# Linear attention and a balanced expert layer: the attention's TensorE work put in the order in which its loads arrive

## The chip, the cores and the metric

The kernel runs on one NeuronCore of a Trainium2 chip. The metric is the device time in microseconds (us) of one execution. The engines of the core work side by side: TensorE (PE, matrix products; its weight loads are shown as PEld), VectorE (DVE), ScalarE (ACT), GpSimd (POOL) and SyncE (SP), whose queue issues the large transfers. TensorE writes to PSUM, and VectorE and ScalarE take results from there to SBUF.

## The reference

Two blocks follow one another. Batch 8, 8 heads, 576 positions, head size 64; all inputs are float32.

```python
kv = np.einsum('bhsd,bhse->bhde', k, v)
out = np.einsum('bhsd,bhde->bhse', q, kv)
rms = np.sqrt(np.mean(out * out, axis=-1, keepdims=True) + 1e-06)
x = (out / rms * g_norm)            # then (batch, head, position, d) -> (batch*position, head*d): 4608 x 512

logits = x @ w_gate                 # 4608 tokens, 8 experts
# tokens are given to experts in the order of all logits, largest first,
# with room for 4608 / 8 = 576 tokens at each expert
for e in range(E):
    h = np.maximum(x[mask_e] @ w1[e], 0.0)     # w1: 512 x 1024
    out[mask_e] = h @ w2[e]                    # w2: 1024 x 512
```

## The kernel before, in words

**Stages.** First the attention for all eight batches, which leaves the normalised rows in a DRAM buffer `x_dram` and the logits in SBUF (`lg`). Then a search for the first expert's threshold, then eight experts one after the other. The change concerns the attention alone.

**Loads.** q, k and v of a batch come in two halves each (`load`, L83): half h has the heads of pairs 2h and 2h+1, 576 KB. All are issued on SP's queue. `paced` (L75) makes each transfer of that queue wait for the one issued three before it, so three are under way at a time. Each half has two buffers, so a batch's buffers serve the batch two later: `again` (L381) issues the load of batch b+2 where the last reader of batch b is issued. The first two batches are loaded at the kernel's start in the order of L92.

**Preparing a batch** (`Prepare`, L373). A pair of heads is one "r" of four.
- `sum_kv` (L406): for each pair 18 matmuls in four 64x64 quadrants (36 records, since each float32 product is two passes) into `kv_ps`; even blocks of positions are summed on one half of the partitions, odd ones on the other.
- `add_halves` (L416): ScalarE copies the odd half (`odd`), VectorE adds it to the even half (`kv`), and GpSimd copies `kv` to both halves of the partitions of `kvx`.
- `turn` (L386): 18 transposes of q, in groups of four (the last, group 4, of two), into a PSUM tile with tag "tr" (two buffers), then a copy to `qt`: groups 1 and 2 by VectorE, 0, 3 and 4 by ScalarE.
- `turn_kv` (L426) transposes kv, in the free half of group 4's PSUM tile, and ScalarE copies that to `kvt`.
- `gate` (L434) multiplies `kvt` with the gate's weights `gw` (already scaled by `g_norm`); eight matmuls, since the result is needed on both halves of the partitions. It lies in free columns of the tile's own PSUM buffer. `keep_gate` (L440) copies it into the last 8 columns of each head in `kvx`: one product with q then gives a head's output and its share of the logits together.

**A group of tiles.** A batch has four tiles of 128 positions, and every second batch a fifth, whose two halves of rows belong to two batches (the "split row": its matmuls are 64x64). `product` (L505) makes one tile, 8 matmuls (16 records) into `o_ps` (two buffers); `square` (L526) squares on ScalarE and sums on VectorE; `keep` (L533) copies the tile to `o_sb`. At the end of the group `scale` and `logits` take the root and the reciprocal, sum the logits, and let GpSimd scale the rows (`xo`) for the write to `x_dram`.

**Order.** The queues of TensorE, VectorE, ScalarE and SP are in the order in which the code issues (`manual_schedule`, L582). `prepare_first` (L445) prepares batch 0. In the loop over the batches, `between` (L462) puts steps of the next batch, and the sums of the one after that, behind each tile: behind the first tile pair 2 and transposes 0, behind the second pair 3, the addition and transposes 1, behind the third transposes 2 and 4 with kv's, and pair 0 of the batch after; the gate comes with the fourth tile (n == 3), transposes 3 and pair 1 behind the last. `ones(n)` (L358) issues n matmuls of 128x128 on 512 columns of ones, whose result nobody reads. `chore` (L352) issues the next piece of small VectorE work for the later search. `writes` holds the transfers to `x_dram`.

Of the kernel before, what the change touches and what calls it, by code (L numbers as in the profile page):

```python
# [7 lines left out]
FT = mybir.dt.float32  # L8
# [7 lines left out]
P = 128  # L16
# [10 lines left out]
def kernel(  # L27
# [24 lines left out]
    W = D + E  # L52
# [12 lines left out]
    att = att_cm.__enter__()  # L65
# [17 lines left out]
    def load(name, b, h):  # L83

        loaded[name, b, h] = att.tile([P, NP // 2, R, D], FT, name=f"{name}_sb", tag=name + str(h), bufs=2)
        rs = slice(h * NP // 2, (h + 1) * NP // 2)
        src = {"k": k, "v": v, "q": q}[name]
        paced(nc.sync.dma_start(
            loaded[name, b, h].rearrange("p r j d -> p r (j d)"),
            src[b].rearrange("h s d -> (h s) d").rearrange("(r p j) d -> p r (j d)", r=NP, j=R)[:, rs]))  # L90

    for b, order in enumerate(("kvqkvq", "kvkvqq")):  # L92
        for n, name in enumerate(order):
            load(name, b, int(name in order[:n]))

# [7 lines left out]
    gw = const.tile([P, NP, 2, E], FT, name="gw")  # L103
# [125 lines left out]
    for st in range(1, NSTEP):  # L229
        n = (1.0 + 2 * FUZZ) / (NCAND + 1) if 1 < st <= DIGITS else 1.0 / (NCAND + 1)  # L230
# [4 lines left out]
    for st in range(1, NSTEP):  # L235
        n = (1.0 + 2 * FUZZ) / (NCAND + 1) if st <= DIGITS else 1.0 / (NCAND + 1)
# [131 lines left out]
    kv_ps = psa.tile([P, 2, 512], FT, name="kv_ps", tag="kv")  # L368
    odds = kv_ps[D:P, :, 0:NP * D]
    evens = kv_ps[0:D, :, 0:NP * D].rearrange("p l (r d) -> p l r d", d=D)  # L370
    OW = NP * W

    class Prepare:  # L373

# [11 lines left out]
        def turn(self, *which):  # L386
            NT = NP * R // 2
            if self.qt is None:
                self.qt = turned_q[self.b] = att.tile([P, 2, NT, HP], FT, name="qt", tag="qt", bufs=2)
            for n in which:  # L390
                m = min(4, NT - 4 * n)
                q_ps = pst.tile([P, 4, P], FT, name="qt_ps", tag="tr")
                for x in range(m):
                    h, at = divmod(4 * n + x, NT // 2)
                    nc.tensor.transpose(q_ps[:, x, :], self.q_sb[h][:, at * P:(at + 1) * P], ident)  # L395
                if n == 4:
                    self.turn_kv(q_ps[:, m:4])
                to, got = self.qt[:, :, 4 * n:4 * n + m], q_ps[:, 0:m].rearrange("p x (l c) -> p l x c", l=2)
                if n in (1, 2):
                    nc.vector.tensor_copy(to, got)  # L400
                else:
                    nc.scalar.copy(to, got)
                if n in (2, 3):
                    self.again("q", n - 2)

        def sum_kv(self, *which):  # L406
            for r in which:
# [18 lines left out]
        def turn_kv(self, beside):  # L426

            t_ps = beside.rearrange("p x c -> p (x c)").rearrange("p (r d) -> p r d", d=D)
            for r in range(NP):
                nc.tensor.transpose(t_ps[:, r, :], self.kv[:, r].rearrange("p l d -> p (l d)"), ident[0:D, 0:D])  # L430
            self.kvt = att.tile([P, NP, D], FT, name="kvt", tag="kvt")
            nc.scalar.copy(self.kvt, t_ps)

        def gate(self, beside):  # L434
            for r in range(NP):
                for n in range(2):
                    nc.tensor.matmul(beside[n * D:(n + 1) * D, r // 2, OW + r % 2 * 2 * E:OW + (r % 2 + 1) * 2 * E],
                                     lhsT=self.kvt[:, r, :], rhs=gw[:, r].rearrange("p l e -> p (l e)"), start=True, stop=True)

        def keep_gate(self, beside):  # L440
            nc.scalar.copy(self.kvx[:, :, D:W].rearrange("p (b h) e -> p b h e", b=2),
                           beside[:, :, OW:OW + NP * E].rearrange("p b (h e) -> p b h e", e=E))
            kv_of[self.b] = self.kvx

    def prepare_first():  # L445

        one = Prepare(0)
        one.sum_kv(0, 1)
        ones(2)
        one.turn(0)  # L450
        ones(6)
        one.sum_kv(2, 3)
        one.add_halves()
        one.turn(1)
        ones(5)
        one.turn(4, 2, 3)
        nc.vector.tensor_scalar(gw.rearrange("p r l e -> p (r l e)"), in0=gw.rearrange("p r l e -> p (r l e)"),
                                scalar1=g_col, scalar2=None, op0=AL.mult)
        one.gate(kv_ps)
        one.keep_gate(kv_ps)  # L460

    def between(n, one, two, count):  # L462

        first = one.b == 1
        if n == 0:
            if first:
                ones(2)
                one.sum_kv(0, 1)
            else:
                one.sum_kv(2)  # L470
                one.turn(0)
        elif n == 1:
            if first:
                one.sum_kv(2)
            one.sum_kv(3)
            one.add_halves()
            one.turn(0 if first else 1)
        elif n == 2:
            if first:
                one.turn(1)  # L480
            one.turn(2, 4)
            if two:
                two.sum_kv(0)
        if n == count - 1:
            one.turn(3)
            if two:
                two.sum_kv(1)

    HELD = 6
    writes, late = [], []  # L490
# [90 lines left out]
    PE, DVE, ACTE, SPE = (mybir.EngineType.PE, mybir.EngineType.DVE, mybir.EngineType.Activation, mybir.EngineType.SP)  # L581
    with tc.manual_schedule(engines={PE, DVE, ACTE, SPE}):  # L582
        ones(18)
        prepare_first()
        preparing = {1: Prepare(1)}
        for b in range(B):
            following = preparing.pop(b + 1, None)
            if b + 2 < B:
                preparing[b + 2] = Prepare(b + 2)
            rows = [((b, j), (b, j + 2)) for j in (0, 1, 4, 5)]  # L590
            if b % 2:
                rows.append(((b - 1, R - 1), (b, R - 1)))
            product, square, keep, scale, logits = tiles(b // 2 * R + b % 2 * (R // 2), rows)
            if b in choose_at:
                early(*choose_at[b])
            order = range(len(rows)) if b % 2 == 0 else [len(rows) - 1] + list(range(len(rows) - 1))
            for n, t in enumerate(order):
                at_end = n if b + 1 == B else 0
                o_ps = product(t, 1 if b == 0 and n in (0, 3) else 0, at_end)
                if following and n == 3:  # L600
                    following.gate(o_ps)
# [12 lines left out]
            logits()  # L614
            if b < 4:
                chore()

            while b in (B - 4, B - 3) and writes:
                writes.pop(0)()
        early(27, GC)  # L620
        while chores:
            chore()
        for do in late:
            do()
        while writes:
            writes.pop(0)()
# [21 lines left out]
    for nm, shape in (("n", (E, G)), ("all", (3, E)), ("a", (GC + 2,)), ("s", (NB, GC + 3))):  # L648
        n = shape[0] * (shape[1] if len(shape) > 1 else 1)
# [737 lines left out]
```

## Time and profile before

| | |
|---|---|
| median of 3 runs | 645.37 us (643.71 to 659.32) |
| the profiled execution's own time | 648.04 us |
| its span, first to last instruction | 646.3 us |
| mean granted TensorE clock | 0.956 |
| attention: first tile, start of the last group, last tile's end | 19.3, 108.2, 113.3 us |
| start of the experts' dense stage | about 150 us |
| TensorE busy, 41 to 63.9 us | 22.9 of 22.9 us |
| HBM read, written | 71.3 MB, 18.9 MB |

The profile's page is of one execution. A "slice" is a fortieth of the span, 16.2 us. "PEclk" is the clock that TensorE was granted, in tenths of full speed. In a timeline each row is a run of like instructions, with its start, its length, the engine, the line, output and inputs, the number, and in brackets the engine's idle time before it with what ended that. "issue" there is idle time that no semaphore explains. Rows of neighbouring groups overlap by about 0.07 us, as the ends of matmuls are modelled; the distance from start to start is the cost of a group.

### The profile page before, as it was taken

To read this page: it belongs to the slowest core of one execution; us is meant where nothing else is said; L and a number is where in the kernel's file an instruction comes from. 1 tells how busy PE (TensorE), PEld (TensorE's weight loads), DVE (VectorE), ACT (ScalarE), POOL (GpSimd) and SP (SyncE) were. 2 spreads that over 40 slices of the span, in tenths; PEclk is the share of its full clock that TensorE was granted. 3 is DMA by queue.
4 is the path that set the end of the run, shared out by engine and by line. 5 is a ranking of instruction groups with operands and counts; after the bars stand their busy time and mean duration, and the time that the engine had idled before them with its cause. 6 is when DMAs were issued, how large, how long until landed. Compare 5 with 4: busy or idle time off the path is not lost.

```text
span 646.3 us, 12765 instructions
## 1 busy us (share of the span) xinstructions
PE 606.6 (94%) x4909; PEld 470.3 (73%) x4913; DVE 378.9 (59%) x1234; ACT 203.9 (32%) x440; POOL 385.8 (60%) x402
## 2 busy tenths in 40 slices
PE   8899999339999999999999999999999999999994
PEld 4688888225787678777867786778678777867873
DVE  4356769777887778579658857966662062132101
ACT  1447667932221232213122312231232123122310
POOL 1133553006775598479739873887498579849822
PEclk9869999558999999999999999999999999999998
DMA  8999998338108206310911091017104420910001
GB/s 277 298 318 307 296 319 327 136 112 250 55 19 316 73 2 235 115 59 1 310 57 42 18 316 42 34 61 273 42 32 161 173 73 1 320 54 33 2 9 65
DMA packets 49852, 91.02 MB, mean 141 GB/s; under 512 B 3712, under 2 KB 20096, under 8 KB 49792
## 3 DMA queue, kind: packets, MB, share of 16 engines
q1 hardware_dynamic: 43200, 71.31, 32.3%
q0 software_dynamic: 5888, 18.88, 8.5%
q8 instruction: 39, 0.64, 0.4%
q14 instruction: 21, 0.17, 0.1%
q10 hardware_dynamic: 704, 0.02, 0.1%
HBM read 71.32 MB, written 18.87 MB: 140 GB/s over the span
## 4 chain that ended last, share of the span: by engine, by line
PE 81%; DVE 9%; issue 5%; DMA 2%; ACT 1%; POOL 1%; POOLq 0%; SPq 0%; DVEq 0%; ACTq 0%
PE x_ps L1203 13%; PE x_ps L1163 12%; PE z_ps L1203 9%; PE y_ps L1203 9%; PE y_ps L1163 8%; PE z_ps L1163 7%; PE o_ps L520 4%; PE y_ps L1265 4%; PE kv_ps L411 3%; PE t_ps L1105 3%; PE qt_ps L395 3%; DMA v_sb<-in_v_dram 2%; PE given_ps L717 1%; PE warm_ps L947 1%; PE given_ps L712 1%
## 5 line engine op out<-in xcount | busy, mean ns | idle before, releaser
L1208 ACT COPY h<-x_ps 128x288 f32<-128x288 f32 x93 | 37.2, 400 | 165.9 <-PE x_ps L1203 159.5
L1203 PE MATMUL x_ps<-xs,sw 128*128 128x288 f32 x248 | 71.4, 409 | 0.4 <-DVE xs L1118 0.4
L1130 POOL DMA_INDIRECT out_dram<-y_sb,outs x32 | 31.5, 985 | 56.5 <-DVE y_sb L1301 41.0
L1163 PE MATMUL x_ps<-tw,sh 128*128 128x256 f32 x256 | 61.5, 384 | 0.0
L1203 PEld LDWEIGHTS x_ps<-xs,sw 128*128 128x128 f32 x248 | 46.1, 190 | 13.5 <-issue 1.1
L1110 ACT ACTIVATE xt<-t_ps,g_col 128x512 f32<-128x512 f32 (+3 forms) x41 | 25.8, 635 | 91.4 <-PE t_ps L1105 91.2
L564 POOL TENSOR_TENSOR xo<-o_sb,inv 128x512 f32<-128x512 f32 x27 | 28.4, 1082 | 40.5 <-DVE inv L551 36.3
L1155 POOL TENSOR_TENSOR sh<-hid 128x512 f32<-128x512 f32 x32 | 40.7, 1271 | 19.8 <-ACT hid L1178 19.8
L1163 PEld LDWEIGHTS x_ps<-tw,sh 128*128 128x128 f32 x256 | 47.0, 190 | 7.0 <-issue 0.8
L1091 POOL TENSOR_TENSOR sw<-w_sb 128x256 f32<-128x256 f32 x64 | 46.8, 731 | 7.7 <-PE z_ps L1203 7.3
L1178 ACT ACTIVATE hid<-hid 128x576 f32<-128x576 f32 x64 | 43.8, 686 | 22.7 <-DVE hid L1217 12.6
L1013 POOL DMA_INDIRECT xg<-x_dram,ids x40 | 38.2, 954 | 15.6 <-issue 9.9
L1241 POOL TENSOR_TENSOR tw<-w_sb 128x512 f32<-128x512 f32 x32 | 40.0, 1273 | 6.6 <-DMA w_sb<-in_moe_w_dram 6.6
L520 PE MATMUL o_ps<-kvx,qt 64*128 64x72 f32 (+1 forms) x624 | 40.7, 281 | 0.6 <-issue 0.4
L531 DVE TENSOR_REDUCE ms<-sq 128x8 f32<-128x512 f32 x36 | 24.4, 682 | 26.8 <-ACT sq L530 26.2
L520 PEld LDWEIGHTS o_ps<-kvx,qt 64*128 64x128 f32 (+1 forms) x624 | 35.5, 187 | 4.9 <-issue 3.7
L1203 PE MATMUL z_ps<-xt,sw 128*128 128x288 f32 x128 | 38.0, 414 | 0.0
L1203 PE MATMUL x_ps<-xt,w_sb 128*128 128x288 f32 x124 | 37.3, 415 | 0.5 <-ACT xt L1110 0.5
L1203 PE MATMUL y_ps<-xt,w_sb 128*128 128x288 f32 x128 | 36.8, 408 | 0.0
L1203 PE MATMUL z_ps<-xs,sw 128*128 128x288 f32 x128 | 36.8, 409 | 0.0
L1203 PE MATMUL y_ps<-xs,w_sb 128*128 128x288 f32 x128 | 36.5, 407 | 0.0
L1295 ACT COPY u<-x_ps 128x512 f32<-128x512 f32 x24 | 14.0, 584 | 66.3 <-PE x_ps L1163 52.6
(315 smaller groups left out, 1337.4 us busy)
## 6 DMA issues: line engine op xcount, KB each, us to landing
w_sb<-in_moe_w_dram SPq DMA_DIRECT2D x32, 512.0 KB, 5.6
w_sb<-in_moe_w_dram SPq DMA_DIRECT2D x8, 2048.0 KB, 12.5
k_sb<-in_k_dram SPq DMA_DIRECT2D x16, 576.0 KB, 5.6
v_sb<-in_v_dram SPq DMA_DIRECT2D x16, 576.0 KB, 5.6
q_sb<-in_q_dram SPq DMA_DIRECT2D x16, 576.0 KB, 6.2
x_dram<-xo SPq DMA_DIRECT2D x16, 512.0 KB, 4.1
x_dram<-xo SPq DMA_DIRECT2D x4, 256.0 KB, 3.5
xg<-x_dram,ids POOLq DMA_INDIRECT x40, 5.1
```

The source lines that it names most:

```text
L520: nc.tensor.matmul(o_ps[rows_at, rp, (2 * r2 + l) * W:(2 * r2 + l + 1) * W], lhsT=turned_q[bn][ks, l, block // 2:block // 2 + m].rearrange ...
L564: nc.gpsimd.tensor_tensor(xo[:, t], o_sb[:, t, :, 0:D], inv[:, t * H:(t + 1) * H].rearrange("p (h o) -> p h o", o=1).to_broadcast([P, H, D ...
L1013: tokens = nc.gpsimd.indirect_dma_start(out=xg[0:nr], out_offset=None, in_=x_dram, in_offset=bass.IndirectOffsetOnAxis(ap=ids[0:nr, n:n + ...
L1091: in_order(nc.gpsimd.tensor_tensor(o, x, y, op=op))
L1130: put = nc.gpsimd.indirect_dma_start(out=out, out_offset=bass.IndirectOffsetOnAxis(ap=ids_of[t][0:nr, n:n + 1], axis=0), in_=y_sb[0:nr, :] ...
L1155: in_order(nc.gpsimd.tensor_tensor(o[:, ms], x[:, ms], y[:, ms], op=op))
L1163: nc.tensor.matmul(p_ps[:, n], lhsT=left[:, f, n * P:(n + 1) * P], rhs=right[:, f], start=first, stop=(f == FH - 1), skip_group_check=True)
L1178: nc.scalar.activation(both, both, ACT.Relu)
L1203: nc.tensor.matmul(p_ps, lhsT=lhs[:, r], rhs=rhs[:, r], start=(m in (1, 2, 4, 5) and r == 0), stop=(r == 1), skip_group_check=(m in (6, 7, ...
L1208: nc.scalar.copy(u, p_ps)
L1241: in_order(nc.gpsimd.tensor_tensor(o, x, y, op=AL.subtract))
L1265: nc.tensor.matmul(y_ps[l * nr:(l + 1) * nr], lhsT=hid[:, l * FH + f, a:a + nr], rhs=w2[:, l * FH + f, :], start=(f == 0), stop=(f == FH - 1))
```

## The change

Four things are changed.

1. **Order of batch 0's loads**: k, v, k, v, q, q instead of k, v, q, k, v, q.
2. **Order of the steps**: `between` and the second batch of look-ahead are gone. Behind tile n of a group comes pair n of the next batch (and behind the first tile the present batch's transposes 4); behind the fourth pair the addition. After the last tile's `keep` come transposes 0 and 1, kv's transposes, a wide matmul of ones after even batches, the gate, and transposes 2 and 3, and only then `scale` and `logits`. In odd batches the split row is second instead of first. Batch 0 is prepared in the same order. The second half of q is loaded again behind transposes 4 instead of 3.
3. **The gate**: kv's transposes and the gate have places of their own in the banks of `kv_ps`. `kvt` holds its columns twice, so that one matmul of 128 weight columns gives both halves of the partitions: four matmuls instead of eight.
4. **Chores and writes**: the chores are issued at other tiles, and the first writes to `x_dram` are issued behind the first tile of batch 5 instead of the end of batch 4.

```diff
-    for b, order in enumerate(("kvqkvq", "kvkvqq")):
+    for b, order in enumerate(("kvkvqq", "kvkvqq")):
...
-    OW = NP * W
+    t_ps = kv_ps[:, 0, NP * D:2 * NP * D].rearrange("p (r d) -> p r d", d=D)
+    w_ps = kv_ps[:, 1, NP * D:NP * (D + 2 * E)].rearrange("p (r e) -> p r e", r=NP)
...
-                if n == 4:
-                    self.turn_kv(q_ps[:, m:4])
...
-                if n in (2, 3):
-                    self.again("q", n - 2)
+                if n in (2, 4):
+                    self.again("q", n // 2 - 1)
...
-            self.kvt = att.tile([P, NP, D], FT, name="kvt", tag="kvt")
-            nc.scalar.copy(self.kvt, t_ps)
+            self.kvt = att.tile([P, NP, 2, D], FT, name="kvt", tag="kvt")
+            nc.scalar.copy(self.kvt, t_ps.rearrange("p r (o d) -> p r o d", o=1).to_broadcast([P, NP, 2, D]))
...
+        def gate(self):
+
             for r in range(NP):
-                for n in range(2):
-                    nc.tensor.matmul(beside[n * D:(n + 1) * D, r // 2, OW + r % 2 * 2 * E:OW + (r % 2 + 1) * 2 * E],
-                                     lhsT=self.kvt[:, r, :], rhs=gw[:, r].rearrange("p l e -> p (l e)"), start=True, stop=True)
...
+                nc.tensor.matmul(w_ps[:, r], lhsT=self.kvt[:, r].rearrange("p n d -> p (n d)"),
+                                 rhs=gw[:, r].rearrange("p l e -> p (l e)"), start=True, stop=True)
+            nc.scalar.copy(self.kvx[:, :, D:W], w_ps.rearrange("p r (l e) -> p (r l) e", l=2))
...
         one.sum_kv(0, 1)
         ones(2)
-        one.turn(0)
-        ones(6)
         one.sum_kv(2, 3)
         one.add_halves()
-        one.turn(1)
         ones(5)
-        one.turn(4, 2, 3)
+        one.turn_kv()
+        one.turn(0, 1)
         nc.vector.tensor_scalar(gw.rearrange("p r l e -> p (r l e)"), in0=gw.rearrange("p r l e -> p (r l e)"),
                                 scalar1=g_col, scalar2=None, op0=AL.mult)
-        one.gate(kv_ps)
-        one.keep_gate(kv_ps)
+        one.gate()
+        ones(2)
+        one.turn(2, 3)
+        return one
...
-            order = range(len(rows)) if b % 2 == 0 else [len(rows) - 1] + list(range(len(rows) - 1))
+            order = (0, 1, 2, 3) if b % 2 == 0 else (0, 4, 1, 2, 3)
             for n, t in enumerate(order):
                 at_end = n if b + 1 == B else 0
-                o_ps = product(t, 1 if b == 0 and n in (0, 3) else 0, at_end)
-                if following and n == 3:
-                    following.gate(o_ps)
+                o_ps = product(t, 1 if b < 2 and n in (0, 3) else 0, at_end)
                 square(t, o_ps)
-                if following and n == 3:
-                    following.keep_gate(o_ps)
-                if following:
-                    between(n, following, preparing.get(b + 2), len(rows))
+                if n == 0:
+                    here.turn(4)
+                if following and n < NP:
+                    following.sum_kv(n)
+                    if n + 1 == NP:
+                        following.add_halves()
                 keep(t, o_ps, at_end)
-                if b < 2 or b == 6 or n in (1, 3):
+                if n + 1 < len(order) and (b < 2 or b == 6 or n in (1, 3)):
                     chore()
-            if b + 1 == B:
+                while (b, n) == (B - 3, 0) and writes:
+                    writes.pop(0)()
+            if following:
+                following.turn(0, 1)
+                following.turn_kv()
+                if b % 2 == 0:
+                    ones(1)
+                following.gate()
+                following.turn(2, 3)
+            else:
                 while chores:
                     chore()
             scale()
             logits()
+            if b % 2 == 0 or b < 2:
+                chore()
             if b < 4:
                 chore()
-            while b in (B - 4, B - 3) and writes:
+            while b == B - 3 and writes:
                 writes.pop(0)()
+            here = following
```

More of the change, by code (lines that the diff above doesn't have):

```diff
@@ L424, in add_halves, with turn_kv @@
                 nc.gpsimd.tensor_copy(self.kvx[n * D:(n + 1) * D, :, 0:D], self.kv.rearrange("p r l d -> p (r l) d"))
-        def turn_kv(self, beside):
-            t_ps = beside.rearrange("p x c -> p (x c)").rearrange("p (r d) -> p r d", d=D)
+        def turn_kv(self):
             for r in range(NP):
                 nc.tensor.transpose(t_ps[:, r, :], self.kv[:, r].rearrange("p l d -> p (l d)"), ident[0:D, 0:D])
-            self.kvt = att.tile([P, NP, D], FT, name="kvt", tag="kvt")
-            nc.scalar.copy(self.kvt, t_ps)
-        def gate(self, beside):
+            self.kvt = att.tile([P, NP, 2, D], FT, name="kvt", tag="kvt")
+            nc.scalar.copy(self.kvt, t_ps.rearrange("p r (o d) -> p r o d", o=1).to_broadcast([P, NP, 2, D]))
+        def gate(self):
             for r in range(NP):
-                for n in range(2):
-                    nc.tensor.matmul(beside[n * D:(n + 1) * D, r // 2, OW + r % 2 * 2 * E:OW + (r % 2 + 1) * 2 * E],
-                                     lhsT=self.kvt[:, r, :], rhs=gw[:, r].rearrange("p l e -> p (l e)"), start=True, stop=True)
-        def keep_gate(self, beside):
-            nc.scalar.copy(self.kvx[:, :, D:W].rearrange("p (b h) e -> p b h e", b=2),
-                           beside[:, :, OW:OW + NP * E].rearrange("p b (h e) -> p b h e", e=E))
+                nc.tensor.matmul(w_ps[:, r], lhsT=self.kvt[:, r].rearrange("p n d -> p (n d)"),
+                                 rhs=gw[:, r].rearrange("p l e -> p (l e)"), start=True, stop=True)
+            nc.scalar.copy(self.kvx[:, :, D:W], w_ps.rearrange("p r (l e) -> p (r l) e", l=2))
             kv_of[self.b] = self.kvx
@@ L449, in prepare_first @@
         ones(2)
-        one.turn(0)
-        ones(6)
         one.sum_kv(2, 3)
         one.add_halves()
-        one.turn(1)
         ones(5)
-        one.turn(4, 2, 3)
+        one.turn_kv()
+        one.turn(0, 1)
         nc.vector.tensor_scalar(gw.rearrange("p r l e -> p (r l e)"), in0=gw.rearrange("p r l e -> p (r l e)"),
                                 scalar1=g_col, scalar2=None, op0=AL.mult)
-        one.gate(kv_ps)
-        one.keep_gate(kv_ps)
[L462 to L487, printed above, removed]
+        one.gate()
+        ones(2)
+        one.turn(2, 3)
+        return one
     HELD = 6
@@ L583 @@
         ones(18)
-        prepare_first()
-        preparing = {1: Prepare(1)}
+        here = prepare_first()
         for b in range(B):
-            following = preparing.pop(b + 1, None)
-            if b + 2 < B:
-                preparing[b + 2] = Prepare(b + 2)
+            following = Prepare(b + 1) if b + 1 < B else None
             rows = [((b, j), (b, j + 2)) for j in (0, 1, 4, 5)]
```

## The prediction

> **What bounds the kernel now.** I read the slices of the page first, then the granted clock window by window, then the waits of the load queue, then the timeline of the first 48 us.
>
> ```profile
> PEclk9869999558999999999999999999999999999998
> DMA  8999998338108206310911091017104420910001
> ```
>
> A slice is 16 us. From slice 10 on (about 150 us) TensorE is at full clock and 90% busy or more: that is the expert stage, which the change doesn't touch. The attention is slices 0 to 6. There the transfers are 80 to 90% busy and TensorE too, and in slices 1 and 2 the clock is down. So the change can only move the moment at which the attention ends; everything behind it moves along.
>
> ```profile
> 9.66:13.08 3.41, 2.24 (x30) 1.30 (x34) 0.00 (x0) 0.59 (x1) 0.00 (x0) 1.00 1.03 364
> 23.32:26.73 3.41, 1.66 (x65) 1.48 (x67) 0.69 (x1) 0.60 (x1) 0.00 (x0) 0.96 0.92 274
> 26.73:30.14 3.41, 3.41 (x47) 2.96 (x41) 1.31 (x6) 1.71 (x3) 1.05 (x2) 0.50 0.91 280
> 40.38:43.80 3.41, 3.41 (x94) 3.12 (x86) 2.46 (x11) 1.31 (x3) 1.45 (x2) 0.54 0.97 327
> 60.86:64.28 3.41, 3.41 (x116) 3.08 (x111) 1.21 (x4) 2.25 (x7) 0.82 (x2) 1.00 0.92 320
> 112.06:115.48 3.41, 2.08 (x51) 1.90 (x48) 3.16 (x6) 2.01 (x6) 0.00 (x0) 0.96 1.02 375
> ```
>
> Columns: stretch, its length, busy us of TensorE, weight loads, VectorE, ScalarE, GpSimd, then granted clock, DMA share, GB/s. The clock halves at 26.7 us, just after a window in which TensorE had only 1.66 of 3.41 us of work, and comes back at 43.8 us. A window of 2.24 us (9.66) kept the full clock; one of 2.08 us (112.06) was the second that lost it. **The loss in the first batch is the largest single item**: its tiles take from 19.27 to 41 us, while later groups take 11.2 us each (41.0 to 108.2 us is six of them).
>
> ```profile
> SPq L88 <- DMA q_sb<-in_q_dram: 24.1, 14, 3.4
> SPq L88 <- DMA k_sb<-in_k_dram: 23.5, 16, 2.7
> SPq L88 <- DMA v_sb<-in_v_dram: 22.0, 15, 2.3
> ```
>
> The load queue waits nearly only for earlier loads (70 us), so loads run at the rate of the transfers, one of 590 KB each 1.95 us. From the issues, the last half of q of batch 7 lands at about 97.5 us, but TensorE starts the last group only at 108.2 us: **TensorE is behind the loads by 10 us and sets the end**.
>
> ```profile
> 12.76 1.38 PE L411 MATMUL kv_ps<-v_sb,k_sb 64*64 64x64 f32 x72 [1.08 <-DMA v_sb<-in_v_dram]
> 14.19 0.58 ACT L418 COPY odd<-kv_ps 64x512 f32<-64x512 f32 x1 [3.19 <-PE kv_ps L411]
> 14.80 0.68 DVE L420 TENSOR_TENSOR kv<-kv_ps,odd 64x512 f32<-64x512 f32 x1 [7.35 <-ACT odd L418]
> 18.22 0.65 PE L437 MATMUL kv_ps<-gw,kvt 128*64 128x16 f32 x16
> 26.12 1.51 PE L411 MATMUL kv_ps<-v_sb,k_sb 64*64 64x64 f32 x48 [1.75 <-issue]
> 49.19 1.11 PE L520 MATMUL o_ps<-kvx,qt 64*128 64x72 f32 x16
> 50.23 0.64 PE L437 MATMUL o_ps<-gw,kvt 128*64 128x16 f32 x16
> 50.81 1.11 PE L520 MATMUL o_ps<-kvx,qt 64*128 64x72 f32 x16
> 51.85 0.66 PE L395 MATMUL qt_ps<-ident,q_sb 128*128 128x128 f32 x4
> 52.44 0.80 PE L411 MATMUL kv_ps<-v_sb,k_sb 64*64 64x64 f32 x36
> 53.17 1.11 PE L520 MATMUL o_ps<-kvx,qt 64*128 64x72 f32 x16
> ```
>
> The last rows are a stretch with no gap at all: start to start, a tile (L520) costs 1.05 us, a pair of heads (L411) 0.73, four transposes (L395) 0.59, the gate (L437) 0.58. That is what a schedule that hides every eviction looks like. The gap at 26.12 us has no semaphore behind it.
>
> [...] the half clock lasts 17.07 us, five windows of 3.41. [...] the gate's 64-column loads run at 0.58 us for 16, the tile's 128-column ones at 1.05 for 16. [...] The page's instruction queue q8 has 39 packets and 0.64 MB, 16 KB each; so the gap of 1.75 us without a releaser is probably a block that came late among the loads. No row proves it.
>
> **The change part by part.**
>
> *Loads of batch 0.* The second v half becomes the fourth load instead of the fifth. The fourth landed at 11.3 us (the issue of load 7), the fifth at 12.7 (where L411 starts). Sums of pairs 2 and 3: 11.3 to 12.7, 1.4 us sooner. But the fill between is cut from 8 wide matmuls and four transposes to 2 wide ones, and TensorE is idle from about 9.7 to 11.3.
>
> *Preparing batch 0.* From 12.7: odd copy and add end at 14.15 (1.4 later, as at 14.19 to 15.48); four kv transposes 0.4; turns 0 and 1, 1.2, to 15.9. The copy of turn 1 is VectorE's (0.67), the scaling of gw comes behind it (0.25), and the gate needs gw: 16.9. Gate 0.5, two wide ones 0.4, turns 2 and 3 1.2: first tile at about 19.2. Before: 19.27. The gain is eaten by putting q behind kv: **nothing**.
>
> *Gate.* 16 loads of 64 columns become 8 of 128: 8 x 65 ns = 0.52 against 0.58. Worth 0.05 us a batch. The copy to kvt grows from 256 to 512 columns: 0.37 to 0.59 us (L402's row for 512), on the path of the gate.
>
> *Group ends.* This is the price. Now turn 0, turn 1, kv transposes, gate, turns 2 and 3 stand in a row behind the last pair's sums, with no tile between. Count from the end of those sums: odd copy and add 1.4 us, covered by turns 0 and 1 (1.2), which leaves 0.3 of idle with hand-overs. Kv transposes 0.4. Then the kvt copy, 0.6 with its hand-over, uncovered but for 0.2 of a wide one after even batches: 0.67 (0.45 even). The copy of turn 3 and the first tile's second half: 0.1. Sum **0.85 us even, 1.07 odd**; bounds 0.5, if the copies overlap as pipelined ones do, and 1.5, if ScalarE still holds the last tile's copy (0.65) ahead of them. The GpSimd copies of kv into kvx (2 x 0.64) end before the gate does; without that cover they would add up to 0.6.
>
> *Sum of the groups.* Two groups: 8 tiles 8.4, the split row 0.55 (33 of its matmuls between 63.7 and 64.4 us beside a pair's), 8 pairs 5.84, 36 transposes 5.3, kv transposes 0.8, gates 1.05, one wide 0.2, stalls 1.92: 24.1 us, against 22.4 now. The loads take 23.4 for two (12 x 1.95), so TensorE remains the bound, and the later release of q's second half (behind the next group's first tile) costs nothing: its buffer is due 10 us later.
>
> Group 0, if the clock stays full: 4 tiles, 2 fills 0.44, 4 pairs, transposes, stalls: 12.2; the data are there (q of batch 1 lands at 27.2, needed at 29). Group 1 starts at 31.5 instead of 41.0: **-9.5**. Groups 1 to 6: 3 x 24.1 + 0.44 of fills + 1.7 of waits without releaser as they stand in this trace after 64 us (0.55, 0.41, 0.27, 0.47) = 74.4, against 67.2: **+7.2**. The last group starts at 105.9 against 108.2: -2.3. Its tiles, chores and the writes to x_dram keep their order (these start behind the last load, at 92 us, in both).
>
> Against the profiled execution (span 646.3, its own time 648.0): 648.0 - 2.3 = **645.7 us**. The median of the runs is 645.4, 2.7 below the profiled one; whether they had less of the half clock isn't shown, so I leave the number as it stands, and let the case reach from 640 (stalls of 0.5, and the 2.7) to 649.
>
> **The rivals.** *The half clock comes back once* (as it did): idle at 9.7 to 11.3 leaves 1.8 to 2.1 us of work in some windows of 3.41, below the 2.24 that was survived; a late instruction block at 24 us would do the same. For it: as many instructions are run by 24 us as before. Against: the five wide ones behind. Then the 8.5 us won from full clock (half of 17) are lost: 654, between 649 and 657.
>
> *The half clock stays.* A group end has 2.34 us of work in 3.41 (odd), 0.1 above the survivor. Once down, the kernel got its clock back only in the window at 40.38, with two pairs and the split row in it; in the new order a pair alternates with a full tile, and that mixture occurs once in two groups. A group at half clock costs 9 us more; from two groups on it is slower than before by more than 2%: +8.5 +9 gives 663, between 657 and 685. It decides when the idle time at group ends passes about 1.2 us.
>
> *The change does less than it says*: TensorE follows the loads, no stalls: the last q lands at 97.5, last group at 98.8, end 9 sooner: 636 to 640.
>
> **How the numbers follow.** Forecast (full clock, stalls paid) 0.42; half clock once 0.33; half clock stays 0.20; at the loads' pace 0.05. Two per cent, 12.9 us, is about what a measurement of this kernel can tell from no change. Under 632.5: 0.02. Above 658.3: the staying half clock, 0.19, and the worst of the single one, 0.01: 0.20. Within: 0.78. Range 640 to 665: leaves out some 0.05 below and 0.10 above, and with it the ends of the cases.
>
> **What would show it.** Right: clock 1.00 from 13 to 110 us; first group in 12.2 us; idle TensorE of about 0.3 and 0.5 to 0.7 around the kv transposes of each group; last tile at about 111. Wrong: stretches of clock 0.5 behind 13 us, or no idle at group ends.

## The result, and the profile after

The changed kernel takes 668.38 us (median of 5 runs, 665.22 to 680.76), the kernel before 643.71 beside it: a ratio of 1.036, interval 1.029 to 1.043. It is slower by 3.6%, where 645.7 was forecast. The time is that of the rival "the half clock stays" (663, 657 to 685). The ratios here leave out runs in which far more half clock fell than in a kernel's fastest; the medians hold every run.

The profiled execution after has 672.71 us, a span of 670.9 and a mean clock of 0.924 (0.956 before). Its slices:

```profile
PEclk8975597855899999999999999999999999999998
```

Before, the clock was down in two of the attention's slices, 1 and 2 (counted from 0); now it is at 0.7 or less in slices 2, 3, 4 and 6 and falls again in 7, and the attention is 25.65 us longer: its last tile ends at 135.36 + 3.62 = 138.98 us, against 113.33. That is the whole loss: from there to the end both profiles have 532 to 533 us.

The same view as before, window by window (stretch, length, busy us of TensorE, weight loads, VectorE, ScalarE, GpSimd, granted clock, DMA share, GB/s):

```profile
9.67:13.08 3.41, 1.58 (x73) 1.40 (x74) 0.00 (x0) 0.16 (x1) 0.00 (x0) 0.96 1.01 364
30.15:33.57 3.42, 2.71 (x21) 2.09 (x20) 1.54 (x3) 2.12 (x5) 1.22 (x2) 0.96 0.95 310
40.40:43.81 3.41, 2.10 (x52) 1.67 (x52) 1.40 (x15) 1.13 (x2) 0.98 (x1) 0.96 0.98 371
64.28:67.70 3.42, 3.42 (x61) 3.05 (x56) 0.93 (x2) 0.77 (x2) 0.00 (x0) 0.50 0.55 209
77.94:81.35 3.41, 3.41 (x96) 3.29 (x89) 3.14 (x7) 1.25 (x3) 2.97 (x3) 0.54 0.59 173
84.76:88.18 3.42, 2.52 (x29) 2.14 (x25) 2.14 (x4) 2.82 (x6) 1.21 (x2) 1.00 0.84 248
98.41:101.83 3.42, 2.62 (x22) 2.25 (x21) 1.24 (x3) 1.56 (x4) 1.21 (x2) 0.96 0.86 261
125.73:129.14 3.41, 2.61 (x21) 2.06 (x20) 1.20 (x3) 1.74 (x4) 1.21 (x2) 0.96 0.90 339
```

The clock fell five times before the attention's end: at 13.09 us (behind the gap before the fourth load), 33.57, 101.84 and 129.14 (each behind a group end), and at 43.81. It was at half for 3.4, 3.4, 37.6, 6.8 and, up to the last tile, 9.8 us: 61 us against 17.07. A clock of 0.96 marks a window whose last moment is already at half: the windows here are set some 0.25 us behind the clock's own record. Some 20 of the 61 us began behind a group end; the longest stretch, 37.6 us, began behind the wait of 1.31 us at 42.20, which no semaphore explains (see below). Note 30.15: TensorE was busy for 2.71 of 3.42 us there and lost the clock, while 84.76 with 2.52 kept it. And 64.28 was busy for all of it and did not bring the clock back. **Busy time doesn't decide.**

The load queue no longer waits only for earlier loads:

```profile
SPq L88 <- DMA k_sb<-in_k_dram: 21.4, 13, 3.2
SPq L88 <- PE kv_ps L410: 17.7, 6, 5.4
SPq L88 <- PE qt_ps L396: 16.9, 9, 4.4
```

Some 35 us of its waits are now for TensorE to free a buffer, so the loads are even less the bound than before.

TensorE in the timeline, rows picked out: the start with the long waits, a group end at half clock, one at full clock of an odd batch and one of an even batch, the last tiles.

```profile
11.50 1.38 PE L410 MATMUL kv_ps<-v_sb,k_sb 64*64 64x64 f32 x72 [1.84 <-DMA v_sb<-in_v_dram]
20.51 1.19 PE L488 MATMUL o_ps<-kvx,qt 64*128 64x72 f32 x16
23.78 0.36 PE L211 MATMUL g_ps<-g,ones_f 128*128 128x8 f32 x2 [0.98 <-DVE ones_f L132]
42.20 0.47 PE L410 MATMUL kv_ps<-v_sb,k_sb 64*64 64x64 f32 x17 [1.31 <-issue]
...
69.54 0.69 PE L428 MATMUL kv_ps<-ident,kv 64*128 64x64 f32 x4
...
70.90 1.89 PE L435 MATMUL kv_ps<-gw,kvt 128*128 128x16 f32 x8
72.62 1.95 PE L396 MATMUL qt_ps<-ident,q_sb 128*128 128x128 f32 x8
...
86.30 0.46 PE L428 MATMUL kv_ps<-ident,kv 64*128 64x64 f32 x4
87.66 1.06 PE L435 MATMUL kv_ps<-gw,kvt 128*128 128x16 f32 x8 [0.90 <-ACT kvt L430]
88.57 1.07 PE L396 MATMUL qt_ps<-ident,q_sb 128*128 128x128 f32 x8
...
98.86 0.46 PE L428 MATMUL kv_ps<-ident,kv 64*128 64x64 f32 x4 [0.45 <-DVE kv L419]
...
100.00 1.06 PE L435 MATMUL kv_ps<-gw,kvt 128*128 128x16 f32 x8 [0.35 <-ACT kvt L430]
...
135.36 3.62 PE L488 MATMUL o_ps<-kvx,qt 64*128 64x72 f32 x32
```

The first tile starts at 20.51. At an odd group's end the gate waits 0.90 us for kvt (0.67 was priced for this wait, 1.07 for the whole group end), and then takes 0.91 from start to start (87.66 to 88.57), where 0.52 was reckoned; at half clock 1.7. The whole group from 56.23 to 76.42 us (its transposes 4 to those of the next group) took 20.2 us at half clock; a group at full clock takes about 12.5 (measured in the kernel with ones, below).

**What the clock goes with.** In both profiles, before and after, every stretch between two changes of the granted clock is a whole number of windows of 3.413 us (3.41, 6.83, 17.07, 20.48, 34.13 and 37.55 us among them). I worked out, for each such window, how much of the array its matmuls used: rows times columns of each matmul as a share of 128x128, times its moving columns, times 0.42 ns a column in bf16 (512 columns of ones are 0.216 us apart) or 0.84 in float32 (288 columns are 0.243 us apart in the expert stage), over 3.41 us. Over 384 windows between 9 and 121 us of thirteen profiled executions (both kernels, the changed one twice, and experiments below), a share of 0.365 or more was followed by the full clock and less by the half clock in 373; the 11 others lie near that bound, most at shares of 0.34 to 0.39. The best bound on busy time gets 289 right. The bound was fitted to these same windows, and a share is good to some 0.03, by how matmuls at a window's edge are counted. The reckoning has a limit: in the kernel with ones in the search (below), four windows of the search, 125.8 to 139.4 us, have shares of 0.26 to 0.32 by it and kept the full clock. Most matmuls there move 8 columns; why the reckoning fails for them isn't shown.

| window of the kernel after | clock in it, next | TensorE busy | array share |
|---|---|---|---|
| 9.67 wait for the fourth load | full, half | 1.58 | 0.34 |
| 30.15 end of the first group | full, half | 2.71 | 0.34 |
| 40.40 with the wait at 42.20 | full, half | 2.10 | 0.31 |
| 64.28 tiles and pairs in turn | half, half | 3.42 | 0.30 |
| 77.94 split row and pairs | half, full | 3.41 | 0.40 |
| 84.76 end of an odd group | full, full | 2.52 | 0.38 |
| 98.41 end of an even group | full, half | 2.62 | 0.31 |

### The profile page after: what moved, and what is told of

It is laid out like the page before. It is cut to its first block, busy times and chain, and to the rows that moved or that the text cites. A ratio compares the mean times of both kernels' runs of the same rounds, so it can differ in the third digit from the quotient of the medians.

```text
span 670.9 us, 12640 instructions
## 1 busy us (share of the span) xinstructions
PE 627.8 (94%) x4849; PEld 490.0 (73%) x4849; DVE 382.0 (57%) x1234; ACT 206.5 (31%) x440; POOL 385.4 (57%) x402
## 4 chain that ended last, share of the span: by engine, by line
PE 81%; DVE 7%; issue 4%; ACT 2%; DMA 2%; POOL 1%; POOLq 0%; DVEq 0%
PE x_ps L1179 13%; PE x_ps L1139 11%; PE z_ps L1179 9%; PE y_ps L1179 8%; PE y_ps L1139 7%; PE z_ps L1139 7%; PE o_ps L488 7%; PE y_ps L1241 4%; PE kv_ps L410 4%; PE qt_ps L396 3%; PE t_ps L1081 3%; PE kv_ps L435 2%; PE given_ps L693 1%; DMA v_sb<-in_v_dram 1%; PE given_ps L688 1%
## 5 line engine op out<-in xcount | busy, mean ns | idle before, releaser
L488 PE MATMUL o_ps<-kvx,qt 64*128 64x72 f32 (+1 forms) x624 | 49.8, 327 | 0.0
L488 PEld LDWEIGHTS o_ps<-kvx,qt 64*128 64x128 f32 (+1 forms) x624 | 44.2, 230 | 4.9 <-issue 3.4
L423 POOL COPY kvx<-kv 64x512 f32<-64x512 f32 x16 | 9.8, 614 | 53.5 <-DVE kv L419 47.3
```

What stands on the lines that cost most here:

```text
L488: nc.tensor.matmul(o_ps[rows_at, rp, (2 * r2 + l) * W:(2 * r2 + l + 1) * W], lhsT=turned_q[bn][ks, l, block // 2:block // 2 + m].rearrange ...
```

## The experiments

All of them compute the whole result; where ones are added, that is work whose result nobody reads. "Half clock" is 2 x (1 - mean clock) x span of a run. In the profiles 35 to 40 us of it lie in the search and at the end, except with ones in the search (15).

| kernel | median us (runs) | ratio to the kernel before | half clock, median us |
|---|---|---|---|
| before (in the last set of runs) | 646.26 (44) | | 49 |
| changed | 668.38 (5) | 1.036 [1.029, 1.043] | 92 |
| changed, again | 670.78 (6) | 1.035 [1.030, 1.040] | 93 |
| changed, ones in the group ends | 656.97 (4) | 1.017 [1.010, 1.025] | 50 |
| changed, transposes 2 ahead of the gate | 655.07 (5) | 1.015 [1.008, 1.021] | 63 |
| changed, gate of before | 652.75 (13) | 1.004 [1.000, 1.008] | 55 |
| the same, again | 650.97 (22) | 1.007 [1.004, 1.010] | 52 |
| gate of before, two early gaps closed | 653.84 (22) | 1.005 [1.002, 1.009] | 58 |
| gate of before, transposes 2 ahead | 664.87 (6) | 1.022 [1.016, 1.029] | 74 |
| all three | 660.00 (6) | 1.022 [1.017, 1.027] | 68 |
| gate of before, transposes 2, more ones | 657.01 (6) | 1.017 [1.012, 1.021] | 59 |
| before, with the doubled gate | 655.15 (21) | 1.004 [1.000, 1.008] | 65 |
| before, with the new load order | 650.98 (4) | none | 59 |
| before, ones in the search | 651.24 (6) | 1.011 [1.006, 1.017] | 32 |

**Ones in the group ends** (of the changed kernel, and in its wait for the fourth load). Work is added to the waits; nothing is taken away.

```diff
-        ones(2)
+        ones(8)
...
+                idle = psa.tile([P, 2, 512], FT, name="o_ps", tag="o", bufs=2)
+                ones(2, idle[:, 0, :])
                 following.turn_kv()
-                if b % 2 == 0:
-                    ones(1)
+                ones(3, idle[:, 0, :])
```

> The changed kernel with wide matmuls of ones where TensorE waits at the group ends (2 ahead of kv's transposes, 3 ahead of the gate instead of 1 in even batches) and in the gap of batch 0 (8 instead of 2). They do no useful work. Theory 1 (half clock: the windows at the group ends hold too little work for the array): the clock stays full from 6 to about 110 us save for a window after a wait without releaser, the last tile ends at 111 to 118 us instead of 139, and the time is 643 to 652. Theory 2 (the loss is TensorE's own longer path at the group ends, the clock only follows): the fills lie in the waits or add up to 1 us a group, and the time stays at 666 to 675.

Measured: 656.97, between the ranges of the two theories, and some 12 us less than the changed kernel by added work alone. In the slices and timeline of this kernel the half clock stands once, behind a wait that no semaphore explains:

```profile
PEclk9979999857999999999999999999999999999997
```

```profile
39.89 1.12 PE L410 MATMUL kv_ps<-v_sb,k_sb 64*64 64x64 f32 x27 [2.18 <-issue]
```

No group end lost the clock; the last tile ended at 121.8 us instead of 139.0. Two groups at full clock took 12.35 + 12.63 = 25.0 us. So at least 12 of the 25 us are half clock, and work in these waits keeps it away. The other half stays: the longer groups, 25.0 us for two where the prediction counted 22.4 before, and whatever the ones cost.

**Transposes 2 ahead of the gate** (of the changed kernel), real work in the same wait.

```diff
+                following.turn(2)
                 following.gate()
-                following.turn(2, 3)
+                following.turn(3)
```

> The changed kernel with transposes 2 ahead of the gate instead of behind it: the wait for the copy of kvt (0.35 us in even, 0.9 in odd batches) is filled with work that has to be done anyway. Theory 2 (path length): 7 x 0.35 to 0.9 = 4.5 us less, 664. Theory 1 (half clock): the same 4.5 us, and in addition the windows at the group ends hold a tenth more work, so part of the half clock goes: 645 to 662, with less half clock than the 61 us of the changed kernel before 139 us.

Measured: 655.07 in the median, as much won as by the ones, but two of the five runs took 673, as long as the changed kernel, with about 100 us of half clock. In the median it shrinks from 92 to 63 us.

**The doubled gate alone** (of the kernel before).

```diff
-                for n in range(2):
-                    nc.tensor.matmul(beside[n * D:(n + 1) * D, r // 2, ...],
-                                     lhsT=self.kvt[:, r, :], rhs=gw[:, r]..., start=True, stop=True)
+                nc.tensor.matmul(beside[:, r // 2, ...],
+                                 lhsT=self.kvt[:, r].rearrange("p n d -> p (n d)"), rhs=gw[:, r]..., start=True, stop=True)
```

> The kernel before with the doubled gate operand alone (four matmuls of 128 weight columns instead of eight of 64, in the old place). The prediction priced it at 0.52 us against 0.58; the changed kernel's trace shows 0.91. If that size belongs to the operation and not to its place, the gate costs 0.33 us more in each of 8 batches: 2.7 us, 646 to 648. If it came from the new place behind the copy, 643 to 645.

Measured: 1.004 [1.000, 1.008] by the ratio, some 2 us, as an operation that costs 0.33 us more would give, but not clear of nothing. The median of the 21 runs, 655.15, lies above both forecasts, with a half clock of 65 us against 49. What is shown is the gate itself: in the old place, too, it takes 0.91 us from start to start.

```profile
33.76 1.06 PE L436 MATMUL o_ps<-gw,kvt 128*128 128x16 f32 x8
34.67 0.64 PE L395 MATMUL qt_ps<-ident,q_sb 128*128 128x128 f32 x4
```

So an edit that halves the number of matmuls makes the gate slower. Why is seen where the two gates are taken record by record. The gate of the kernel before (number, then min/median/max in ns, first and last start):

```profile
L437 PEld LDWEIGHTS o_ps<-gw,kvt x16: 133/138/138, 50.2 to 50.6; 128*64 128x64 f32 x16
```

The gate of the changed kernel at full clock:

```profile
L435 PEld LDWEIGHTS kv_ps<-gw,kvt x8: 186/192/192, 87.7 to 88.4; 128*128 128x128 f32 x8
```

Sixteen old loads need less time than eight new ones. In the trace's records the old loads start in pairs: at 50.518 and 50.524 us, 50.576 and 50.583, a pair every 58 ns, the two loads of a pair having 64 columns each, one for each half of the result's partitions. The new ones start one at a time, every 111 ns. So two loads of 64 columns had been under way at once already; doubling the operand puts 128 columns into one load and takes that away.

**The new load order alone** (of the kernel before, with batch 0 prepared in the order of the loads).

```diff
-    for b, order in enumerate(("kvqkvq", "kvkvqq")):
+    for b, order in enumerate(("kvkvqq", "kvkvqq")):
...
-        one.turn(0)
-        ones(6)
...
-        one.turn(1)
...
-        one.turn(4, 2, 3)
+        one.turn(4, 0, 1)
...
+        ones(2)
+        one.turn(2, 3)
```

> The kernel before with the new order of batch 0's loads and the preparation of batch 0 in the order of the changed kernel, the rest as before. Theory 1: the gap at 9.7 to 11.4 us costs the full clock for a window from 13 us on, the first tile comes at 20 instead of 19.3, later half clock by chance as before: 643 to 650. If this order is what loses the time: 655 or more.

Measured: 643.93, 658.02, 658.89 and 643.80 us. Slices of the first one:

```profile
PEclk8899999559999999999999999999999999999998
```

The half clock comes twice for one window (12.7 and 19.5 us) and then not until the search. The order of the loads is not what makes the changed kernel slow, and these four runs show no gain from it.

**The gate of before** (in the changed kernel, otherwise untouched).

```diff
-            self.kvt = att.tile([P, NP, 2, D], FT, name="kvt", tag="kvt")
-            nc.scalar.copy(self.kvt, t_ps.rearrange("p r (o d) -> p r o d", o=1).to_broadcast([P, NP, 2, D]))
+            self.kvt = att.tile([P, NP, D], FT, name="kvt", tag="kvt")
+            nc.scalar.copy(self.kvt, t_ps)
...
-                nc.tensor.matmul(w_ps[:, r], lhsT=self.kvt[:, r].rearrange("p n d -> p (n d)"),
-                                 rhs=gw[:, r].rearrange("p l e -> p (l e)"), start=True, stop=True)
+                for n in range(2):
+                    nc.tensor.matmul(w_ps[n * D:(n + 1) * D, r], lhsT=self.kvt[:, r, :],
+                                     rhs=gw[:, r].rearrange("p l e -> p (l e)"), start=True, stop=True)
```

> The changed kernel with the gate of the kernel before (eight matmuls of 64 weight columns, kvt of 256 columns), in the new place. Theory (the doubled operand costs 0.35 us more a batch, and its 0.9 us are a stretch in which the array does next to nothing, so it brings the half clock): 2.8 us from the operation itself, and a part of the half clock too: 650 to 664. If the place alone matters: 664 to 668.

and, on one chip with a later repair,

> The new order with only the gate of before, again, on the same chip as the kernel with its gaps closed: 645 to 655; the difference between the two is what the two early places cost.

Measured: 652.75 and 650.97. By the medians this one part of the change carries 16 to 20 of its 25 us, most of it by way of the half clock: the gate's own time is 0.33 us in each of eight batches. Slices of the second, and its end of an even group:

```profile
PEclk9789999758999999999999999999999999999998
```

```profile
84.00 0.46 PE L428 MATMUL kv_ps<-ident,kv 64*128 64x64 f32 x4 [0.45 <-DVE kv L419]
84.39 0.39 PE L363 MATMUL ones_ps<-wide,ones_b 128*128 128x512 bf16 x1
84.92 0.65 PE L436 MATMUL kv_ps<-gw,kvt 128*64 128x16 f32 x16
85.49 1.09 PE L396 MATMUL qt_ps<-ident,q_sb 128*128 128x128 f32 x8
```

The wait for kv (0.45) is still there; the gate is back at 0.57 us. Array shares at its group ends are 0.39 to 0.47, and the clock holds at all of them that are reached at full clock: half clock only at 24.7 to 38.4 us. Two groups, their waits without a releaser taken out, take 11.81 + 12.1 = 23.9 us.

**The gate of before, and transposes 2 ahead of it; more ones as well; two early places closed.** Four repairs built on the last kernel.

```diff
+                following.turn(2)
                 following.gate()
-                following.turn(2, 3)
+                following.turn(3)
```

> The new order with the gate of before (eight matmuls of 64 weight columns, kvt 256 columns) and transposes 2 ahead of the gate, so that they stand in its wait; no further fill. If the loss comes from group ends in which the array does too little, because of the wait and of a gate of 0.91 us: no group end loses the clock at full clock, the half clock before the attention's end shrinks from 61 us to under 30, and the time is 642 to 654. If the order itself holds TensorE's path long (waits and sums, whatever the clock): groups at full clock stay at 12.3 us or more and the time is above 655. Two groups at full clock should take 23.3 to 23.8 us.

With ones(2) ahead of kv's transposes, ones(1) ahead of the gate and ones(8) in the wait for the fourth load besides:

> The changed kernel with all three mended: the gate of before, transposes 2 ahead of the gate, and wide matmuls where TensorE still waits (2 ahead of kv's transposes, 1 ahead of the gate, 8 in the first gap). Two groups then cost 23.3 us at full clock, against 25.0 with fills alone and 22.4 before. If half clock, gate and waits are the whole loss, the kernel is within 1% of the one before: 640 to 652. If something else of the change costs time (chores, writes, order of the loads), it stays at 655 or more.

Transposes 2 ahead, and the two early places closed without other ones:

```diff
-    for n in range(0, len(set_up), 5):
-        chores.append(lambda n=n: [do() for do in set_up[n:n + 5]])
+    for n in range(-2, len(set_up), 5):
+        chores.append(lambda n=n: [do() for do in set_up[max(n, 0):n + 5]])
...
-        ones(2)
+        ones(8)
```

> As the kernel with old gate and transposes 2 ahead of it, and two places in the first 25 us closed as well: eight wide matmuls of ones in place of two in the wait for the fourth load, and the set-up chores cut so that the first one issues three operations instead of five. If thin windows are the whole cause: no half clock at 13 us nor at 23 us; what is left comes from waits without a releaser; 638 to 650. If the fills only push the path: the first tile later than 20.5 us and no gain over the kernel without them.

The two early places alone, with transposes 2 where the change has them:

> The new order with the gate of before, transposes 2 behind the gate as in the changed kernel, and the two early places closed (eight wide matmuls in the wait for the fourth load, the first set-up chore three operations). If what is left of the loss is half clock from thin windows: as the kernel with the old gate alone or 3 to 8 us better, 640 to 650; no half clock at 23 us. If transposes 2 ahead of the gate were what made the last two repairs slow: groups at full clock of 11.8 to 12.0 us here against 12.1 there. If the new order's longer path sets the time: not below 645.

The changed kernel beside them:

> The changed kernel again, on the same chip as its repairs: 665 to 672 us, about 20 us above the kernel before. If half of the half clock is the price, a run's time is about 622 us and half of its time at half clock, as in the runs before.

Measured: 664.87, 657.01, 660.00 and 653.84: none is better than the gate of before alone, and all four medians lie above their expectation. Half of each was right. With transposes 2 ahead, no group end lost the clock, and the half clock before the attention's end shrank from 61 to 27 us; but two groups take 12.1 + 11.9 = 24.0 us, not 23.3 to 23.8. Closing the early places did remove the 0.98 us wait of L211 and the half clock behind it. Each of the four also has a wait with no semaphore behind it, 1.32, 2.43, 2.40 and 2.22 us long, at another place in each, and the half clock from there. In the timeline of the last:

```profile
90.67 0.21 PE L410 MATMUL kv_ps<-v_sb,k_sb 64*64 64x64 f32 x1 [2.22 <-issue]
```

Its window has an array share of about 0.15, and the half clock lasted for 20.5 us. Why the kernels with transposes 2 ahead are slower than those without stays open: groups at full clock are as long, and they had more half clock in all their runs (62, 51 and 47 us at the least with, 36 without).

The runs of the kernel with the early places closed that had the least half clock, 36 to 37 us, took 644.3 to 646.1 us (5 runs, mean 645.4); those of the kernel before beside it with 38 us or less, 641.8 to 645.3 (10 runs, mean 643.5).

**Ones in the search** (of the kernel before, 28 at one step of the first search and 5 behind each later one's small product):

```diff
+                    if s == 0 and c == 27:
+                        warm(28)
...
+            if first and not last:
+                warm(5)
```

> The kernel before, with wide matmuls of ones in the search for the first threshold (28 ahead of the last third of the first count, 5 behind each step's small product), where TensorE waits for VectorE and the clock is half for 34 us in every trace. If half clock there costs time on the path: the counts of 36 small matmuls take 0.6 to 0.8 us instead of 1.15 to 1.45, 3 us in all, 639 to 644. If the fills come into the path instead: 646 to 650.

Measured: 651.24, above both forecasts. The half clock falls to 32 us in the median and the kernel is slower by 1.1%. In its profile the time behind the attention is 537.8 us against 532.9 in the kernel before: the ones cost more there than the fast clock won.

## Why the prediction was wrong

**What bounds it, and where the loss lies: right.** TensorE sets the attention's end, the loads follow it, and behind the attention nothing moved.

**Loads of batch 0: right; what follows them: 1.2 us short.** Sums of pairs 2 and 3 start at 11.50 (11.3 foreseen), after a wait of 1.84 us. The first tile came at 20.51, not 19.2: the clock was already at half from 13.09 to 16.50, and the gate took 0.9. A loss of 1.2 in place of nothing.

**Gate: wrong.** "8 x 65 ns = 0.52" took the tile's figure, 1.05 us for 16 loads of 128 columns. But those have 64 rows, and in the kernel before they start in pairs, a pair every 112 ns (49.739 and 49.746 us, 49.851 and 49.858), as the old gate's loads of 64 columns do every 58; the old gate's matmuls start in pairs too, 6 to 7 ns apart. The new gate's loads, of 128 rows and 128 columns, have no partner: they measured 111 ns each, and the gate 0.91 us, 0.39 a batch more than the price.

**Group ends: right, to 0.2 us.** Foreseen 0.3 before kv's transposes, 0.45 (even) and 0.67 (odd) before the gate; measured 0.45 and 0.35 in an even group, 0 and 0.90 in an odd one: 0.8 and 0.9 against 0.85 and 1.07.

**Sum of the groups: right but for the gate.** Foreseen 24.1 us for two; 23.9 with the gate of before, 25.0 with the new one.

**Chores cost nothing: wrong by about 1 us.** L211 waits 0.98 us for VectorE's first set-up chore (0.22 before).

**The clock: the step that failed.** "A group end has 2.34 us of work in 3.41 (odd), 0.1 above the survivor" judged by busy time. The group ends had more than that, 2.61 and 2.71 us of busy time, and lost the clock, since the waits, the gate (by the same reckoning 0.11 us of the array's time in 0.91) and kv's transposes (0.11 in 0.39) fill a window without filling the array: shares of 0.31 to 0.34. That put the likeliest case on full clock. What the runs showed in its place is the share of the array as the measure, with a bound near 0.365, and 61 us of half clock. The rival that came true named the rest rightly: the group end as the place, the mixture of tile and pair that can't bring the clock back (0.30), the odd group that can (split row and pairs, 0.40), and the price of a group at half clock (7.7 us measured, 9 foreseen). Its deciding point was wrong: 1.2 us of idle time were not needed, 0.8 were enough together with the thin gate. Part of the size is chance: the stretch of 37.6 us began behind a wait without a releaser (see below), and the prediction named a late block only for its rival "once". In the second profile of the changed kernel 27 of 55 us began behind group ends, and 24 behind the wait of L211.

The sum, from the forecast's end of the last tile (about 111) to the measured 139.0, against the terms foreseen: first tile +1.3; seven groups 7 x 12.5 = 87.5 for 84.9, +2.6, which is the gate; last tiles +0.3; waits of L211 and without a releaser, 2.3 for 1.7, +0.6; and the half clock +23.2, which is what is left. It agrees with the groups one by one, each less 12.5 us and those waits: +2, +5.3, +7.7, +2, +0.7, +1.8, +0.8 and the last tiles +2.8: 23. Twenty-three of twenty-eight us are the clock.

**Was the forecast's case a real one?** With the clock kept, nearly: the new order with the gate of before and the two early places closed ran in 644.3 to 646.1 us when it had 36 to 37 us of half clock, about what lies behind the attention, beside 645.7 foreseen. But the 8.5 us that the prediction set against the waits were no steady gain. At 0.4 us for each us of half clock, 17 us are worth 6.8. And the kernel before, too, has 38 us or less in 10 of the 44 runs, and is then 2 us faster by the means.

**The waits without a releaser.** The prediction took the one it saw for a late instruction block, and said that no row proves it. The traces' records of single packets point the same way. The attention has sixteen such waits of 1.07 to 2.43 us, in eleven of the fourteen profiled executions. Each ended 1.24 to 1.50 us after a packet of 16 KB on the instruction queue (q8) had landed: the one at 42.20 us, for example, 1.24 us after a packet that landed at 40.96, and the one at 26.12 us in the kernel before 1.43 us after one at 24.69. And each stands at the same place in the count of TensorE's records: 186 to 194 past a multiple of 256 (190 and 193 for these two; the kernel before has 39 such packets for 10,038 records, 257 each). From these two regularities I take the waits to be for late blocks; no record names the cause. They were priced as 1.7 us of path; the one at 42.20 us had a stretch of 37.6 us of half clock behind it besides.

**Open.** Why such a wait comes in one execution and not in another, and why transposes 2 ahead of the gate didn't help. Nor was each of the smaller parts tried alone: the chores, the writes, the later load of q, the place of the split row.

## What to carry to other kernels

Before you merge two matmuls into a wider one, look whether their records start in pairs: here nothing was gained by joining loads that already ran side by side, and the gate with eight wide loads took 0.91 us where sixteen narrow ones had taken 0.58. Where work with few rows, few columns or short moving operands is gathered into one place, add up its share of the array over each 3.41 us window and not its busy time; in this kernel's attention half clock came behind windows with less than about 0.365 (373 of 384 windows lay on their side of that bound), and windows of 0.40 ended it (77.94). Ask whether the work that follows is as dense as that. A forecast of a few stalls is worth nothing until that second sum is made.

## What the runs showed of the hardware

- In the attention of these kernels the clock went with the share of the array that was used in windows of 3.41 us, with one bound near 0.365 in both directions (373 of 384 windows). Fully busy windows stayed at half clock (64.28: 3.42 of 3.42 us) and windows with a fifth idle lost it (30.15: 2.71 of 3.42): busy time doesn't tell. Transposes had to be counted by their size like other matmuls: leaving them out of the share makes 101 windows wrong instead of 11.
- A stretch of half clock cost about 0.4 of its length: a straight line through the runs has a slope of 0.39 for the kernel before (44 runs), 0.40 and 0.41 for two of the repairs (22 runs each). A group at half clock, 20.2 us for 12.5, lost 0.38 of its own; the gate's wait of 0.35 us at 100.00 (full clock) is gone at 70.90 (half clock).
- Added work made the kernel faster: with ones whose result nobody reads, in waits of 0.4 to 0.9 us and in the wait for the fourth load, it took 656.97 us where the changed kernel took 668.38, some 12 us less.
- TensorE stood for 1.07 to 2.43 us without a semaphore to explain it while the loads ran, sixteen times in fourteen executions; each wait ended 1.24 to 1.50 us after a 16 KB packet had landed on the instruction queue.
